# A fused attention and mixer kernel: the last group's output add split in two, its last two down-projection steps ordered by block, and a 64-row matmul operand widened to 128 rows with zeros

## The chip, the cores and the metric

The kernel runs on one core of one Trainium2 chip. The metric is the device time of one execution in microseconds (us), the median of several runs. The core has a matrix engine (TensorE, PE in the profile, with its weight loads shown apart as PEld), a vector engine (VectorE, DVE), a scalar engine (ScalarE, ACT), a general engine (GpSimd, POOL) and a queue that starts transfers (SyncE, SP). Every engine takes its own instructions in order and waits at semaphores for the others.

## The reference

Eight sequences of 576 tokens go through attention with 8 heads of 64 channels, four heads with a local mask of 32 tokens and four with a strided one, and then through two mixers:

```
x  = attention output, [8, 576, 512]
h  = relu(x^T @ w_tok1) @ w_tok2          # token mix: 576 -> 256 -> 576, over tokens
u  = x + h^T
h2 = relu(u @ w_ch1) @ w_ch2              # channel mix: 512 -> 1536 -> 512
out = u + h2
```

## The kernel before

**Precision.** Every matmul of the mixers is made of three. An operand `a` is held as a rounded part and a remainder, `ah + al`, both in a format that TensorE takes at one pass, and a product is `ah*bh + ah*bl + al*bh`. So names come in pairs: `t1h/t1l` are the weights of token mix 1, `w1h/w1l` and `w2h/w2l` those of the channel mix, `xh/xlo` are an activation, `uh/ul` are u, `gh/gl` the hidden layer. The rounded parts are written by ScalarE, the remainders by VectorE or GpSimd.

**Token mix 1 (`tok1`, L374).** For one sequence it contracts over the 576 tokens in `NSC` = 5 chunks of 128 rows. For each chunk, ScalarE makes `xh` (L384), VectorE `xlo` (L387), and TensorE does three matmuls for each of the two halves `m` of the 256 outputs (L396). The fifth chunk is short: 64 tokens are left. Its 64 rows of x are loaded twice, into rows 0 to 63 and 64 to 127. `t1l` holds for this chunk the rounded weights in its upper rows and the remainders in its lower rows, so that one matmul of 128 rows gives two of the three products; the third, rounded weights with `xlo`, is a matmul of 64 rows. `t1h` of that chunk has the rounded weights in all 128 rows, though only the first 64 are used there. It runs nine times: for sequence 0 in two halves of 256 columns, in the first part of the kernel, and for sequences 1 to 7 with 512 columns. ScalarE (`hh`, L400) and VectorE (`hl`, L404) read its result.

**Channel mix (`mlp`, L513).** The 8 x 576 tokens are taken in `NG` = 9 groups of 512. In a group, `up_proj` (L524) does 12 matmuls for each of `NFC` = 12 blocks `fc` of the hidden layer, ScalarE and VectorE make `gh` and `gl` (L528, L530), and `down_proj` (L538) adds 12 matmuls into the four accumulators `acc0` to `acc3`, one for each block of 128 output channels, all four in PSUM. At the end of a group the outputs are put together block by block (L559 to L563): VectorE adds acc and `uh` into a buffer `ot` of which there are two, then `ul` is added, by GpSimd or in the last group by VectorE, and SP stores the block of 256 KB.

**Order.** The first part of the kernel, with the conversion of the weights and group 0, follows an order written out by hand. After that the attention of the next sequences, their token mixes and the channel mix of the group before are woven together: functions are hung on half steps of the channel mix (`inserts`), and a scheduler that goes by its own time estimates and by priorities sets the final order on each engine. The strided attention runs as products on GpSimd (L342, L359) and sums on VectorE (L343, L361); its result goes through memory into `x`, of which there is one buffer. From group 7 on little but the channel mix is left.

Of the kernel before, what the change touches and what calls it, by code (L numbers as in the profile page):

```python
# [10 lines left out]
F32 = mybir.dt.float32  # L11
# [4 lines left out]
ALU = mybir.AluOpType  # L16
# [9 lines left out]
P = 128  # L26
# [6 lines left out]
NCC = DM // P  # L33
NFC = DF // P
NSC = 5
# [8 lines left out]
GT = 512  # L44
NG = B * S // GT
# [3 lines left out]
def attn_mixer_kernel(ctx, tc, qT, kT, vw, qs, ks, vs, qksT, vsP, mask, mask2, w1, w2, wt1, wt2, outT):  # L49
    nc = tc.nc  # L50
# [11 lines left out]
    w2h = const.tile([P, NFC, DM], F32R, name="w2h")  # L62
    w2l = const.tile([P, NFC, DM], F32R, name="w2l")

    t1h = const.tile([P, NSC, DT], F32R, name="t1h")
    t1l = const.tile([P, NSC, DT], F32R, name="t1l")
# [12 lines left out]
    def differ(name):  # L79
        return nc.gpsimd if name in ON_GPSIMD.split() else nc.vector  # L80


    def convert(name, srcs, n, cut):

        raw = stage.tile([P, DM, 2], U32, name="w_raw", bufs=3)
        for r0, c0, src in srcs:
            nr, w = src.shape
            nc.sync.dma_start(out=raw[r0:r0 + nr, c0:c0 + w].rearrange("p n t -> p (n t)"), in_=src.bitcast(U32))
        yield
        a = stage.tile([P, DM], U32, name="w_f", bufs=2)[:, :n]  # L90
        low, high = raw[:, :n, 0], raw[:, :n, 1]

        nc.scalar.activation(out=a.bitcast(F32), in_=high.bitcast(F32), func=AF.Abs, scale=REBIAS)
        if name in BY_VECTOR.split():
            yield
            nc.vector.tensor_scalar(out=a, in0=a, scalar1=3, scalar2=None, op0=ALU.logical_shift_left)
            nc.vector.scalar_tensor_tensor(out=a, in0=low, scalar=29, in1=a, op0=ALU.logical_shift_right, op1=ALU.bitwise_xor)
            nc.vector.scalar_tensor_tensor(out=a, in0=high, scalar=0x80000000, in1=a, op0=ALU.bitwise_and, op1=ALU.bitwise_xor)
        else:


            octets = raw.rearrange("p n t -> p (n t)").bitcast(U8).rearrange("p (n e) -> p n e", e=8)
            nc.scalar.copy(out=octets[:, :n, 4], in_=octets[:, :n, 3])
            yield
            nc.vector.tensor_scalar(
                out=high, in0=high, scalar1=5, scalar2=0x80000007, op0=ALU.arith_shift_right, op1=ALU.bitwise_and)
            nc.vector.scalar_tensor_tensor(out=a, in0=a, scalar=3, in1=high, op0=ALU.logical_shift_left, op1=ALU.bitwise_xor)
        yield
        yield from cut(a.bitcast(F32))

    def split(name, dsth, dstl, *srcs):
        c0, got = 0, []
        for src in srcs:
            got.append((0, c0, src))
            c0 += src.shape[1]

        def cut(f):
            if len(dsth.shape) == 3:
                f = f.rearrange("p (c n) -> p c n", c=dsth.shape[1])
            nc.scalar.copy(out=dsth, in_=f)  # L120
            yield
            differ(name).tensor_tensor(out=dstl, in0=f, in1=dsth.bitcast(F32), op=ALU.subtract)

        return convert(name, got, c0, cut)

    def t1_pieces():
        for c in range(0, NSC - 1, 2):
            yield split(f"t{c // 2}", t1h[:, c:c + 2], t1l[:, c:c + 2], *(wt1[P * i:P * i + P] for i in (c, c + 1)))

        def cut(f):  # L130
            nc.scalar.copy(out=t1h[:, NSC - 1], in_=f)
            nc.scalar.copy(out=t1l[:64, NSC - 1], in_=f[:64])
            yield
            differ("t2").tensor_tensor(out=t1l[64:, NSC - 1], in0=f[64:], in1=t1h[64:, NSC - 1].bitcast(F32), op=ALU.subtract)


        short = wt1[P * (NSC - 1):]
        yield convert("t2", [(0, 0, short), (64, 0, short)], DT, cut)
# [236 lines left out]
    def tok1(pool, banks, x_t, h, cs):  # L375

        n = cs.stop - cs.start
        ph = [b[:, cs] for b in banks]

        def chunk(c):  # L380
            short = c == NSC - 1
            x = x_t[:, c, cs]
            xh = pool.tile([P, DM], F32R, name="xh")[:, :n]
            nc.scalar.copy(out=xh, in_=x)  # L384
            yield
            xlo = pool.tile([P, DM], F32R, name="xlo")[:, :n]
            nc.vector.tensor_tensor(out=xlo, in0=x, in1=xh.bitcast(F32), op=ALU.subtract)  # L387
            yield
            for m in range(2):
                ms = slice(P * m, P * m + P)  # L390
                if short:
                    terms = ((t1h[:64, c, ms], xlo[:64]), (t1l[:, c, ms], xh))
                else:
                    terms = ((t1h[:, c, ms], xh), (t1h[:, c, ms], xlo), (t1l[:, c, ms], xh))
                for k, (l, r) in enumerate(terms):
                    nc.tensor.matmul(ph[m], l, r, start=(c == 0 and k == 0), stop=(short and k == 1), skip_group_check=True)  # L396

        def last():
            for m in range(2):
                nc.scalar.activation(out=h[m][0][:, cs], in_=ph[m], func=AF.Relu)  # L400
            yield
            for m in range(2):
                a, z = h[m][0][:, cs], h[m][1][:, cs]
                nc.vector.scalar_tensor_tensor(out=z, in0=ph[m], scalar=0.0, in1=a.bitcast(F32), op0=ALU.max, op1=ALU.subtract)  # L404

        return [chunk(c) for c in range(NSC)] + [last()]

    def new_h(pool):
        return [[pool.tile([P, DM], F32R, name=f"h{k}{m}", bufs=1) for k in "hl"] for m in range(2)]

    def new_u(pool):
        return [[pool.tile([P, GT], F32R, name=f"u{k}", bufs=NCC) for k in "hl"] for _ in range(NCC)]
# [30 lines left out]
    xp = ctx.enter_context(tc.tile_pool(name="xp", bufs=2))  # L443
# [37 lines left out]
    with tc.tile_pool(name="first", bufs=2) as first, \  # L481
# [4 lines left out]
        us = {0: new_u(xp)}  # L486
# [18 lines left out]
    up = ctx.enter_context(tc.tile_pool(name="up", bufs=3, reuse_waits="tile"))  # L505
# [4 lines left out]
    def run(g, n=100):  # L510
        for _ in range(n):
            next(g, None)

    def mlp(grp, us, inserts):
        acc = [ps_acc.tile([P, GT], F32, name=f"acc{cc}") for cc in range(NCC)]
        g = {}

        def up_proj(fc):
            fs = slice(P * fc, P * fc + P)
            ph = ps_h.tile([P, GT], F32, name="h")  # L520
            for cc in range(NCC):
                uh, ul = us[cc]
                for k, (l, r) in enumerate(((w1h, uh), (w1h, ul), (w1l, uh))):
                    nc.tensor.matmul(ph, l[:, cc, fs], r, start=(cc == 0 and k == 0), stop=(cc == NCC - 1 and k == 2))  # L524
            yield
            gh = up.tile([P, GT], F32R, name="gh")
            gl = up.tile([P, GT], F32R, name="gl")
            nc.scalar.activation(out=gh, in_=ph, func=AF.Relu)  # L528
            yield
            nc.vector.scalar_tensor_tensor(out=gl, in0=ph, scalar=0.0, in1=gh.bitcast(F32), op0=ALU.max, op1=ALU.subtract)  # L530
            g[fc] = (gh, gl)

        def down_proj(fc):
            gh, gl = g.pop(fc)
            for cc in range(NCC):
                cs = slice(P * cc, P * cc + P)
                for k, (l, r) in enumerate(((w2h, gh), (w2h, gl), (w2l, gh))):
                    nc.tensor.matmul(acc[cc], l[:, fc, cs], r, start=(fc == 0 and k == 0), stop=(fc == NFC - 1 and k == 2))  # L538
            yield

        if grp:
            run(up_proj(0))
            run(up_proj(1))
            for fc in range(NFC):
                if fc + 2 < NFC:
                    run(up_proj(fc + 2))
                for f in inserts.get(2 * fc, ()):
                    f()
                run(down_proj(fc))
                for f in inserts.get(2 * fc + 1, ()):  # L550
                    f()
        else:
            for fc in range(NFC):
                steps[f"A{fc}"], steps[f"D{fc}"] = up_proj(fc), down_proj(fc)
            in_order(ORDER.split("|")[1])
            for n, s in steps.items():
                assert next(s, steps) is steps, n
        for cc, (uh, ul) in enumerate(us):
            o_t = up.tile([P, GT], F32, name="ot", bufs=2)  # L559
            nc.vector.tensor_tensor(out=o_t, in0=acc[cc], in1=uh.bitcast(F32), op=ALU.add)  # L560
            add = nc.vector if grp == NG - 1 else nc.gpsimd
            add.tensor_tensor(out=o_t, in0=o_t, in1=ul.bitcast(F32), op=ALU.add)  # L562
            nc.sync.dma_start(out=outT[P * cc:P * cc + P, GT * grp:GT * grp + GT], in_=o_t)  # L563

    def do_load(b):
# [180 lines left out]
```

## Time and profile before

| what | value |
|---|---|
| median of 3 runs | 886.46 us (879.77, 886.46, 888.44) |
| the profiled execution, its own time | 882.51 us |
| its span, first to last instruction | 880.5 us |
| granted TensorE clock, mean | 0.982 |
| TensorE matmuls busy | 826.7 us, 94% of the span |
| VectorE busy | 487.8 us, 55% |
| GpSimd busy | 404.0 us, 46% |
| ScalarE busy | 208.5 us, 24% |

The profile is of one execution, and times within it are us from the first instruction. In a row of the timeline stand start, length, engine, line, operation, the tiles as out<-in, the shape, and in brackets how long the engine was idle before it and whom it waited for. The chain of waits is the work that ended last, followed back from the last instruction; a row has start, length, and engine with line, and xN where N instructions in a row are put together. A matmul's end in the profile is modelled, so its pace is read from the distance of the starts.

### The profile page before, as it was taken

The page shows a single profiled execution, that of the slowest core. Times are in us where ns is not written, and L with a number is a line of the kernel's source. Part 1 is how long each engine was busy: PE and PEld are TensorE (multiplying, and loading weights), DVE is VectorE, ACT ScalarE, POOL GpSimd, SP SyncE. Part 2 cuts the span into 40 slices and gives each one's busy share as a digit, 9 for nine tenths or more (in the row PEclk, how much of TensorE's full clock was granted, in tenths as well). Part 3 has the DMA queues.
Part 4 walks back from the last instruction along what each step waited for, and adds up shares of the span by engine and source line. Part 5 has one row for each costly group of instructions (what it writes and reads, how often), then busy time and mean ns, then how long its engine had stood idle before and what let it go on. Part 6 is the DMA issues. An engine that isn't in the chain of part 4 may idle for free.

```text
span 880.5 us, 16250 instructions
## 1 busy us (share of the span) xinstructions
PE 826.7 (94%) x6820; PEld 659.7 (75%) x6820; DVE 487.8 (55%) x941; ACT 208.5 (24%) x378; POOL 404.0 (46%) x385
## 2 busy tenths in 40 slices
PE   4588999799978999999999999999999999999996
PEld 3366787578856787787887887778788877888885
DVE  4789873667567755775577567645774222112112
ACT  3676652221112212211212112112111121111110
POOL 0112300786577765795679477845885002002000
PEclk9979999999998999999999999999999999999998
DMA  7647754302542323023402421223112001001001
GB/s 256 198 157 251 240 191 123 130 1 92 132 160 63 102 54 123 28 80 88 157 28 79 142 97 40 74 64 115 35 53 77 11 1 48 1 1 41 8 1 48
DMA packets 57639, 78.99 MB, mean 90 GB/s; under 512 B 18144, under 2 KB 39776, under 8 KB 57568
## 3 DMA queue, kind: packets, MB, share of 16 engines
q1 hardware_dynamic: 57568, 77.97, 27.5%
q8 instruction: 53, 0.87, 0.4%
q14 instruction: 18, 0.15, 0.1%
HBM read 59.54 MB, written 18.28 MB: 88 GB/s over the span
## 4 chain that ended last, share of the span: by engine, by line
PE 65%; POOL 13%; DVE 9%; DMA 7%; issue 2%; SPq 2%; ACT 1%; DVEq 0%; POOLq 0%; ACTq 0%
PE h L524 25%; PE acc L538 23%; POOL sprod L342 9%; PE t L433 6%; POOL sprod L359 4%; PE t L396 4%; DMA sb<-in_ks 3%; PE t L427 3%; DVE ss L343 2%; DMA lk<-in_kT 1%; PE t L207 1%; DVE xlo L387 1%; PE t L170 1%; SPq L372 1%; DMA xs<-sb 1%
## 5 line engine op out<-in xcount | busy, mean ns | idle before, releaser
L342 POOL TENSOR_TENSOR sprod<-sb,sa 128x576 f32<-128x576 f32 (+6 forms) x162 | 175.1, 1110 | 133.8 <-DMA sb<-in_ks 114.8
L359 POOL TENSOR_TENSOR sprod<-sa,ss 128x448 f32<-128x448 f32 (+7 forms) x162 | 162.9, 1038 | 34.3 <-DVE ss L352 24.9
L524 PE MATMUL h<-ul,w1h 128*128 128x512 f32 x432 | 170.7, 395 | 0.0
L524 PE MATMUL h<-uh,w1l 128*128 128x512 f32 x432 | 169.5, 392 | 0.0
L538 PE MATMUL acc<-gh,w2l 128*128 128x512 f32 x432 | 169.3, 392 | 0.0
L524 PE MATMUL h<-uh,w1h 128*128 128x512 f32 x432 | 168.4, 396 | 0.9 <-DVE gl L530 0.9
L538 PE MATMUL acc<-gl,w2h 128*128 128x512 f32 x432 | 168.7, 390 | 0.0
L538 PE MATMUL acc<-gh,w2h 128*128 128x512 f32 x432 | 165.6, 394 | 0.2 <-ACT gh L528 0.2
L530 DVE SCALAR_TENSOR_TENSOR gl<-h,gh 128x512 fp32r<-128x512 f32 x108 | 74.0, 686 | 141.5 <-ACT gh L528 141.3
L528 ACT ACTIVATE gh<-h 128x512 fp32r<-128x512 f32 x108 | 64.4, 599 | 317.7 <-PE h L524 304.3
L343 DVE TENSOR_REDUCE ss<-sprod 128x9 f32<-128x576 f32 (+6 forms) x162 | 90.8, 570 | 55.4 <-POOL sprod L342 54.3
L361 DVE TENSOR_REDUCE sb<-sprod 128x64 f32<-128x64 f32 (+8 forms) x162 | 91.4, 571 | 36.9 <-POOL sprod L359 35.9
L562 POOL TENSOR_TENSOR ot<-ot,ul 128x512 f32<-128x512 f32 x32 | 41.2, 1295 | 136.5 <-DVE ot L560 136.4
L524 PEld LDWEIGHTS h<-uh,w1h 128*128 128x128 f32 x432 | 81.0, 188 | 18.4 <-DVE gl L530 1.4
L538 PEld LDWEIGHTS acc<-gh,w2h 128*128 128x128 f32 x432 | 81.2, 188 | 17.6 <-ACT gh L528 0.7
L524 PEld LDWEIGHTS h<-uh,w1l 128*128 128x128 f32 x432 | 81.6, 189 | 16.7
L524 PEld LDWEIGHTS h<-ul,w1h 128*128 128x128 f32 x432 | 81.4, 189 | 16.8
L538 PEld LDWEIGHTS acc<-gh,w2l 128*128 128x128 f32 x432 | 81.1, 188 | 17.1
L538 PEld LDWEIGHTS acc<-gl,w2h 128*128 128x128 f32 x432 | 81.1, 188 | 16.3
L387 DVE TENSOR_TENSOR xlo<-x,xh 128x512 fp32r<-128x512 f32 (+1 forms) x45 | 40.0, 905 | 33.8 <-ACT xh L384 33.7
L438 DVE TENSOR_TENSOR ul<-t,uh 128x512 fp32r<-128x512 f32 (+7 forms) x64 | 28.8, 454 | 42.6 <-ACT uh L436 42.4
L436 ACT CAST uh<-t 128x512 fp32r<-128x512 f32 (+7 forms) x64 | 25.5, 399 | 108.8 <-PE t L433 108.7
(97 smaller groups left out, 881.0 us busy)
## 6 DMA issues: line engine op xcount, KB each, us to landing
w_raw<-in_w SPq DMA_DIRECT2D x24, 512.0 KB
out_t<-ot SPq DMA_DIRECT2D x36, 256.0 KB
lv<-in_vw SPq DMA_DIRECT2D x8, 520.0 KB
x<-xs SPq DMA_DIRECT2D x8, 512.0 KB
lv<-in_vw SPq DMA_DIRECT2D x6, 650.0 KB
xl<-lx SPq DMA_DIRECT2D x14, 256.0 KB
x<-xl SPq DMA_DIRECT2D x7, 512.0 KB
sa<-in_qs SPq DMA_DIRECT2D x6, 576.0 KB
```

What stands on the lines that cost most here:

```text
L342: nc.gpsimd.tensor_tensor(out=pr, in0=k_t[:, n0:n0 + n], in1=q_t[:, i:i + 1].to_broadcast([P, n, D]), op=ALU.mult)
L343: nc.vector.tensor_reduce(out=s_t[:, i, n0:n0 + n], in_=pr, axis=AX.X, op=ALU.add)
L359: nc.gpsimd.tensor_tensor(out=pr, in0=v_t[:, d0:d0 + nd, :n], in1=s_t[:, i:i + 1, :n].to_broadcast([P, nd, n]), op=ALU.mult)
L361: nc.vector.tensor_reduce(out=o_t[:, i, d0:d0 + nd], in_=pr, axis=AX.X, op=ALU.add)
L387: nc.vector.tensor_tensor(out=xlo, in0=x, in1=xh.bitcast(F32), op=ALU.subtract)
L396: nc.tensor.matmul(ph[m], l, r, start=(c == 0 and k == 0), stop=(short and k == 1), skip_group_check=True)
L433: nc.tensor.matmul(pu[:, :n], l[:, cs], r[:, m, t0:t1], start=False, stop=(m == 1 and k == 2), skip_group_check=True)
L524: nc.tensor.matmul(ph, l[:, cc, fs], r, start=(cc == 0 and k == 0), stop=(cc == NCC - 1 and k == 2))
L528: nc.scalar.activation(out=gh, in_=ph, func=AF.Relu)
L530: nc.vector.scalar_tensor_tensor(out=gl, in0=ph, scalar=0.0, in1=gh.bitcast(F32), op0=ALU.max, op1=ALU.subtract)
L538: nc.tensor.matmul(acc[cc], l[:, fc, cs], r, start=(fc == 0 and k == 0), stop=(fc == NFC - 1 and k == 2))
L562: add.tensor_tensor(out=o_t, in0=o_t, in1=ul.bitcast(F32), op=ALU.add)
```

## The change

It has three parts.

One: the conversion of `w_tok1`'s short chunk sets the lower 64 rows of `t1h` to zero after `t1l` has been made from them, and `tok1` then takes all 128 rows of `t1h` and of `xlo` for the third product. The lower rows add zero times x. The number of matmuls stays as it is.

Two: in the last group u is put together ahead of the end, `whole = uh + ul`, one VectorE operation a block at steps 4 to 7. At the end one operation a block adds acc to it, in place, and the store reads from there. `whole` takes the place of the buffer of `x`, which has all four blocks, so no block waits for the store of another.

Three: in the last group the down-projection of the last two steps, `fc` 10 and 11, is one call that goes through the accumulators one after the other, both steps for each.

```diff
@@ conversion of w_tok1, cut() of the short chunk
             differ("t2").tensor_tensor(out=t1l[64:, NSC - 1], in0=f[64:], in1=t1h[64:, NSC - 1].bitcast(F32), op=ALU.subtract)
+            differ("t2").memset(t1h[64:, NSC - 1].bitcast(F32), 0.0)
@@ tok1
                 if short:
-                    terms = ((t1h[:64, c, ms], xlo[:64]), (t1l[:, c, ms], xh))
+                    terms = ((t1h[:, c, ms], xlo), (t1l[:, c, ms], xh))
@@ mlp
-        def down_proj(fc):
-            gh, gl = g.pop(fc)
+        def down_proj(*fcs):
+            gs = [g.pop(fc) for fc in fcs]
             for cc in range(NCC):
                 cs = slice(P * cc, P * cc + P)
-                for k, (l, r) in enumerate(((w2h, gh), (w2h, gl), (w2l, gh))):
-                    nc.tensor.matmul(acc[cc], l[:, fc, cs], r, start=(fc == 0 and k == 0), stop=(fc == NFC - 1 and k == 2))
+                for fc, (gh, gl) in zip(fcs, gs):
+                    for k, (l, r) in enumerate(((w2h, gh), (w2h, gl), (w2l, gh))):
+                        nc.tensor.matmul(acc[cc], l[:, fc, cs], r, start=(fc == 0 and k == 0), stop=(fc == NFC - 1 and k == 2))
...
-                run(down_proj(fc))
+                if grp < NG - 1 or fc < NFC - 2:
+                    run(down_proj(fc))
+                elif fc == NFC - 2:
+                    run(down_proj(fc, fc + 1))
...
+                if grp == NG - 1 and 4 <= fc < 4 + NCC:
+                    if fc == 4:
+                        whole = xp.tile([P, NSC, GT], F32, name="x", bufs=1)
+                    uh, ul = (u.bitcast(F32) for u in us[fc - 4])
+                    nc.vector.tensor_tensor(out=whole[:, fc - 4], in0=uh, in1=ul, op=ALU.add)
...
         for cc, (uh, ul) in enumerate(us):
-            o_t = up.tile([P, GT], F32, name="ot", bufs=2)
-            nc.vector.tensor_tensor(out=o_t, in0=acc[cc], in1=uh.bitcast(F32), op=ALU.add)
-            add = nc.vector if grp == NG - 1 else nc.gpsimd
-            add.tensor_tensor(out=o_t, in0=o_t, in1=ul.bitcast(F32), op=ALU.add)
+            if grp == NG - 1:
+                o_t = whole[:, cc]
+                nc.vector.tensor_tensor(out=o_t, in0=acc[cc], in1=o_t, op=ALU.add)
+            else:
+                o_t = up.tile([P, GT], F32, name="ot", bufs=2)
+                nc.vector.tensor_tensor(out=o_t, in0=acc[cc], in1=uh.bitcast(F32), op=ALU.add)
+                nc.gpsimd.tensor_tensor(out=o_t, in0=o_t, in1=ul.bitcast(F32), op=ALU.add)
             nc.sync.dma_start(out=outT[P * cc:P * cc + P, GT * grp:GT * grp + GT], in_=o_t)
```

The scheduler decides where these instructions stand, and it did not keep the order of the code in part three. First TensorE, the last twelve matmuls of the program. The numbers are the program's: `gh_8569` belongs to the last step, `fc` 11. Before:

```order
L538 MATMUL acc0_8257<-gh_8569,w2h_69 128x512
L538 MATMUL acc1_8258<-gh_8569,w2h_69 128x512
L538 MATMUL acc0_8257<-gl_8570,w2h_69 128x512
L538 MATMUL acc0_8257<-gh_8569,w2l_70 128x512
L538 MATMUL acc1_8258<-gl_8570,w2h_69 128x512
L538 MATMUL acc1_8258<-gh_8569,w2l_70 128x512
L538 MATMUL acc2_8259<-gh_8569,w2h_69 128x512
L538 MATMUL acc2_8259<-gl_8570,w2h_69 128x512
L538 MATMUL acc2_8259<-gh_8569,w2l_70 128x512
L538 MATMUL acc3_8260<-gh_8569,w2h_69 128x512
L538 MATMUL acc3_8260<-gl_8570,w2h_69 128x512
L538 MATMUL acc3_8260<-gh_8569,w2l_70 128x512
```

The same twelve places of the changed kernel, where `gh_8546` is step 10 and `gh_8575` step 11:

```order
L540 MATMUL acc2_8260<-gh_8575,w2h_69 128x512
L540 MATMUL acc3_8261<-gl_8547,w2h_69 128x512
L540 MATMUL acc0_8258<-gl_8576,w2h_69 128x512
L540 MATMUL acc0_8258<-gh_8575,w2l_70 128x512
L540 MATMUL acc1_8259<-gl_8576,w2h_69 128x512
L540 MATMUL acc1_8259<-gh_8575,w2l_70 128x512
L540 MATMUL acc2_8260<-gl_8576,w2h_69 128x512
L540 MATMUL acc2_8260<-gh_8575,w2l_70 128x512
L540 MATMUL acc3_8261<-gh_8546,w2l_70 128x512
L540 MATMUL acc3_8261<-gh_8575,w2h_69 128x512
L540 MATMUL acc3_8261<-gl_8576,w2h_69 128x512
L540 MATMUL acc3_8261<-gh_8575,w2l_70 128x512
```

Counted from the last matmul as 0, the accumulators are complete at 8, 6, 3 and 0 before, and at 8, 6, 4 and 0 in the changed kernel. Only acc2 moved, by one place.

Second, VectorE at the end of the program, where the outputs are put together. Before:

```order
L530 SCALAR_TENSOR_TENSOR gl_8570<-h_8556,gh_8569 128x512
L560 TENSOR_TENSOR ot_8609<-acc0_8257,uh_7892 128x512
L560 TENSOR_TENSOR ot_8613<-acc1_8258,uh_7894 128x512
L562 TENSOR_TENSOR ot_8609<-ot_8609,ul_7893 128x512
L562 TENSOR_TENSOR ot_8613<-ot_8613,ul_7895 128x512
L560 TENSOR_TENSOR ot_8617<-acc2_8259,uh_7896 128x512
L560 TENSOR_TENSOR ot_8621<-acc3_8260,uh_7898 128x512
L562 TENSOR_TENSOR ot_8617<-ot_8617,ul_7897 128x512
L562 TENSOR_TENSOR ot_8621<-ot_8621,ul_7899 128x512
```

The changed kernel there:

```order
L531 SCALAR_TENSOR_TENSOR gl_8576<-h_8562,gh_8575 128x512
L573 TENSOR_TENSOR x_8441<-acc0_8258,x_8441 128x512
L573 TENSOR_TENSOR x_8441<-acc1_8259,x_8441 128x512
L573 TENSOR_TENSOR x_8441<-acc2_8260,x_8441 128x512
L573 TENSOR_TENSOR x_8441<-acc3_8261,x_8441 128x512
```

Eight operations after the last `gl` became four, and each of them waits for TensorE alone; before, the third and fourth L560 also waited for the stores of the first two blocks.

Third, VectorE where the four new additions went. They do not stand in the last group but one group earlier, in group 7, around the last `ul` of token mix 2. Before:

```order
L530 SCALAR_TENSOR_TENSOR gl<-h,gh 128x512 x2
L438 TENSOR_TENSOR ul<-t,uh 128x512
L530 SCALAR_TENSOR_TENSOR gl<-h,gh 128x512
L438 TENSOR_TENSOR ul<-t,uh 128x512 x2
L530 SCALAR_TENSOR_TENSOR gl<-h,gh 128x512
L438 TENSOR_TENSOR ul<-t,uh 128x512
L530 SCALAR_TENSOR_TENSOR gl<-h,gh 128x512 x8
```

In the changed kernel:

```order
L531 SCALAR_TENSOR_TENSOR gl<-h,gh 128x512 x2
L439 TENSOR_TENSOR ul<-t,uh 128x512
L531 SCALAR_TENSOR_TENSOR gl<-h,gh 128x512
L439 TENSOR_TENSOR ul<-t,uh 128x512 x2
L531 SCALAR_TENSOR_TENSOR gl<-h,gh 128x512
L563 TENSOR_TENSOR x<-uh,ul 128x512 x3
L439 TENSOR_TENSOR ul<-t,uh 128x512
L563 TENSOR_TENSOR x<-uh,ul 128x512
L531 SCALAR_TENSOR_TENSOR gl<-h,gh 128x512 x8
```

The first of the four waits for TensorE to have read `x` for the last time, and the last `ul` and eight `gl` stand behind it. On GpSimd the new memset stands right behind the subtraction for `t1l`'s lower rows (L134), and TensorE's first short-chunk matmul waits for it. Every other instruction stands on its engine as before.

## The prediction

> **What bounds the kernel now.** I read the page first, for the busy shares and the chain of waits by engine; then the pieces of that chain in order of time, to see where TensorE sets the end and where not; then the timeline at the two places that the change touches.
>
> ```profile
> PE 826.7 (94%) x6820; PEld 659.7 (75%) x6820; DVE 487.8 (55%) x941; ACT 208.5 (24%) x378; POOL 404.0 (46%) x385
> PE 65%; POOL 13%; DVE 9%; DMA 7%; issue 2%; SPq 2%; ACT 1%; DVEq 0%; POOLq 0%; ACTq 0%
> ```
>
> TensorE is busy for 94% of the span, but only 65% of the chain is TensorE's; GpSimd, VectorE and transfers carry 29%. So time taken from TensorE counts only in the stretches where the chain is TensorE's. At the very end the chain is no longer TensorE's either:
>
> ```profile
> 870.37 0.39 PE L538 MATMUL acc<-gh,w2l 128*128 128x512 f32 x1
> 872.18 0.39 PE L538 MATMUL acc<-gh,w2l 128*128 128x512 f32 x1
> 870.85 1.29 DVE L560 TENSOR_TENSOR ot<-acc,uh 128x512 f32<-128x512 f32 x2 [5.08 <-PE acc L538]
> 872.05 1.28 DVE L562 TENSOR_TENSOR ot<-ot,ul 128x512 f32<-128x512 f32 x2
> 874.89 1.31 DVE L560 TENSOR_TENSOR ot<-acc,uh 128x512 f32<-128x512 f32 x2 [1.55 <-DMA out_t<-ot]
> 876.12 1.28 DVE L562 TENSOR_TENSOR ot<-ot,ul 128x512 f32<-128x512 f32 x2
> 872.76 2.00 DMA out_t<-ot
> 872.50:879.50 7.00, 0.07 (x1) 0.00 (x0) 3.35 (x6) 0.00 (x0) 0.00 (x0) 0.73 0.39 150
> ```
>
> The last matmul starts at 872.18. VectorE does two blocks, then stands idle for 1.55 us until a store (2.00 us) frees one of the two buffers, and does the other two. It ends at 876.12 + 1.28 = 877.40, and the span of 880.5 ends 3.1 us later: the last store, and the program's close.
>
> The other place is the short chunk of token mix 1. This is sequence 7's, first TensorE's matmuls, then its weight loads, then line L396 in five windows, and a piece of the chain for the ordinary pace:
>
> ```profile
> 709.94 0.39 PE L524 MATMUL h<-ul,w1h 128*128 128x512 f32 x1
> 710.26 0.50 PE L396 MATMUL t<-xlo,t1h 64*128 64x512 f32 x1
> 710.69 0.49 PE L396 MATMUL t<-xh,t1l 128*128 128x512 f32 x1
> 711.11 0.50 PE L396 MATMUL t<-xlo,t1h 64*128 64x512 f32 x1
> 711.54 0.50 PE L396 MATMUL t<-xh,t1l 128*128 128x512 f32 x1
> 711.87 0.39 PE L524 MATMUL h<-uh,w1l 128*128 128x512 f32 x1
> 710.68 0.19 PEld L396 LDWEIGHTS t<-xh,t1l 128*128 128x128 f32 x1 [0.25 <-issue]
> 712.10 0.19 PEld L524 LDWEIGHTS h<-ul,w1h 128*128 128x128 f32 x1
> sum 9.66, PE 8.07 PEld 3.69; mean PE 1.61 PEld 0.74
> 766.49 2.72 PE acc L538 x12
> ```
>
> Twelve ordinary matmuls take 2.72 us, 0.227 each. Around the 64-row matmuls the starts lie 0.32, 0.43, 0.42, 0.43 and 0.33 apart. The loads show why: in the ordinary stream a load stands a whole matmul ahead of its own (the one at 712.10 runs beside the matmul that starts there, for the next), but the load of 710.68 starts with its matmul, after 0.25 us in which nothing was loaded. Between a 64-row and a 128-row operand the load does not run ahead, four times a place and a little less at the edges. The sum row is of five such places (sequences 3 to 7), each from the start of the last ordinary matmul before to that of the first one after, five distances: 9.66 / 5 = 1.93 us where 5 x 0.227 = 1.13 would stand. So a place costs **0.80 us** of TensorE.
>
> **The change, part by part.** *The end.* acc0 is complete with the ninth matmul from the last, as before, and VectorE started 870.85 - 870.37 = 0.48 after that matmul's start. The four remaining operations read what L560 read in one operand and SBUF in the other, and pairs of them start 0.6 apart (the two at 870.85 fill 1.29, the second lasting 0.68). So they start at 870.85, 871.46, 872.06 and, for acc3, 872.18 + 0.48 = 872.66, and end at 873.35. That is 877.40 - 873.35 = 4.05 us earlier. What comes behind is the same but for the stores: four now follow each other 0.6 us apart. In the 7 us of the windows' row the transfer engines were busy for a share of 0.39, which is 2.73 us for four stores, 0.68 each; the last may wait for 3 x 0.08 = 0.2 us or so. I take **3.9 us**. Bounds: 3.4 if it waits for a whole store, 4.05 if for none. The store queue is free, since SP has nothing else there. That two steps now alternate on an accumulator costs nothing that a row shows: the stream at 766.49 has three matmuls in a row on each accumulator at the ordinary pace, and the last step's `gh` and `gl` are not asked for earlier than the 14th matmul from the end, 3.0 us before the last start, while the last `gl` of before started at 865.08:
>
> ```profile
> 865.08 0.69 DVE L530 SCALAR_TENSOR_TENSOR gl<-h,gh 128x512 fp32r<-128x512 f32 x1 [4.75 <-ACT gh L528]
> 753.81 0.69 DVE L530 SCALAR_TENSOR_TENSOR gl<-h,gh 128x512 fp32r<-128x512 f32 x1 [1.97 <-ACT gh L528]
> 754.27 0.88 PE t L427 x5
> 755.16 1.59 PE t L433 x6
> 761.72 0.69 DVE L530 SCALAR_TENSOR_TENSOR gl<-h,gh 128x512 fp32r<-128x512 f32 x1 [3.56 <-ACT gh L528]
> 38.36 0.94 POOL L134 TENSOR_TENSOR t1l<-w_f,t1h 64x256 fp32r<-64x256 f32 x1 [7.06 <-ACT t1h L131]
> 48.57 1.54 POOL L122 TENSOR_TENSOR w1l<-w_f,w1h 128x512 fp32r<-128x512 f32 x1 [9.28 <-ACT w1h L120]
> 51.05 0.38 PE L396 MATMUL t<-xlo,t1h 64*128 64x256 f32 x1 [0.62 <-DVE xlo L387]
> ```
>
> *The four additions in advance.* They stand behind the `gl` of 753.81 and wait for TensorE's last reading of `x`, the transposes that end at 755.15, or, if the wait is put at the end of the six matmuls behind them, at about 756.7. Three times 0.69 (L562's pace on VectorE) then end at 757.2 to 758.8; behind them wait the last `ul` and the `gl` of 761.72, before which VectorE was idle for 3.56 us. I cost them at nothing. Their cover goes if they start after about 759.5; then TensorE would be late by what is over.
>
> *The memset.* The subtraction of 38.36 is followed on GpSimd by 9.28 us of idleness, and the first matmul that needs the zeros starts at 51.05, held by VectorE. No row shows a memset of this shape; between 0 and the 0.94 of the subtraction of the same 64x256, either is hidden. I take nothing.
>
> *The short chunk.* If 128 rows put it at the ordinary pace, 0.80 us is saved at each of seven places, and something in the two halves of sequence 0. What of it reaches the end is read from the chain:
>
> ```profile
> 60.77 0.42 DVE L404 SCALAR_TENSOR_TENSOR hl<-t,hh 128x256 fp32r<-128x256 f32 x1 [0.39 <-ACT hh L400]
> 168.83 0.69 DVE ot L560
> 270.45 5.80 PE t L396 x14
> 355.43 1.71 PE t L396 x4
> 442.38 12.59 POOL sprod L342 x9
> 471.63 0.61 DVE gl L530
> 531.08 11.77 POOL sprod L342 x8
> 633.41 1.71 PE t L396 x4
> 450.63:452.57 1.94, 1.62 (x4) 0.74 (x4) 1.00 0.04 8
> 541.32:543.25 1.93, 1.61 (x4) 0.74 (x4) 1.00 0.00 0
> ```
>
> Sequences 2, 3, 6 and 7 have their short chunk on the chain (270.45, 355.43, 633.41, and the matmuls of 710.26, where the chain is TensorE's to the end): 4 x 0.80 = 3.2 us. Sequence 1's lies at 168 us, where VectorE waits for a store with its `ot` (168.83) and the next `hl` stands behind that: nothing. Sequences 4 and 5 have theirs in the windows from 450.63 and 541.32, in the stretches where GpSimd's products carry the chain (442.38, 531.08); TensorE would come sooner to the next wait for VectorE (471.63): nothing. At the end of sequence 0's `tok1` the chain goes on over ScalarE and VectorE, which waited there for 0.39 us (60.77): 0.4. Together **3.6 us**. The bounds: 0, or all of it, 7 x 0.80 = 5.6 and for sequence 0 up to twice 0.80, 7.2.
>
> The sum: 3.9 + 3.6 = **7.5 us**. Against the profiled execution's own 882.51 that is 875.0; the median of the runs shown stands 3.95 above that execution, and from 886.46 it is **879.0 us**, 0.85% faster.
>
> The Trainium skill ("TensorE: Matmul & The Clock Gate", The mechanism) says that a weight load runs beside matmuls in flight only when the two use different row groups of the array. By that rule a 128-row load after a 128-row matmul would be the one that can't run ahead; the row of 712.10 shows it running ahead, so the trace speaks against the rule in this form. By the rule the short chunk would gain nothing and the sum would be 3.9; it is the second rival.
>
> **The rivals.** *All of the chunk's gain arrives.* The chain alternates between engines, and a GpSimd stretch that starts earlier because TensorE came earlier gives everything back to it. Then 3.9 + 7.2 = 11.1: 875.4. Against it, the waits at 471.63 and 168.83, which TensorE's being early does not move.
>
> *The chunk gains nothing.* The gaps could belong to something other than the 64 rows, such as the alternation of `xlo` and `t1l` operands in two halves. For it, the edges of the place (0.32 and 0.33) lie between 128-row operands and 64-row ones and are not doubled. Against it, the ordinary chunks alternate in the same way without a gap. It gives 886.46 - 3.9 = 882.6.
>
> *Slower: VectorE's stretched operations.* An `xlo` on the chain is several times as long as its line's median:
>
> ```profile
> 267.37 3.04 DVE xlo L387
> L387 DVE TENSOR_TENSOR xlo<-x,xh x45: 409/691/3026, 36.2 to 705.1; 128x512 fp32r<-128x512 f32 x35, 128x256 fp32r<-128x256 f32 x10
> ```
>
> The median is 0.69, the longest 3.03: it lies beside a product on GpSimd, and both read SBUF. The change shifts these two engines against each other by up to a microsecond. If four more operations on the chain came to lie so, each 3.03 - 0.69 = 2.3 us longer, they would take 9.4 and the result would be 886.46 - 7.5 + 9.4 = 888.4. It decides from the fourth on (7.5 / 2.3 = 3.2). The one that is there could as well go, for 2.3 us more gain. The Trainium skill ("SBUF — State Buffer", SBUF: two separate sides) says that VectorE with two SBUF inputs and GpSimd take a shared pair of ports in turn, whole instructions at a time; these rows agree, and by it no such operation would wait longer than one product, which gives no other sum.
>
> **How the numbers follow.** My forecast, with some tenths to either side in both terms, has a chance of 0.58; all of the chunk 0.2; nothing of it 0.13; slower 0.04; 0.05 is left for what I don't see. A difference of about 1%, 8.9 us, is what a measurement of this kernel can tell from no change: the three runs of before span 8.7 us by themselves. Faster by more means below 877.6. The second case (875.4) mostly lies there, and the forecast's 879.0 falls there in some two of five measurements, since medians vary by a few us: 0.37 in all. Slower by more needs over 895.3: 0.02. The range takes in 875.4 and 882.6 with some 3 us of the runs' own spread outside of each: 872.5 to 885.0.
>
> **What would show it.** At the end: VectorE's four operations back to back behind TensorE's last matmul, no wait for a store, the span's end some 4.4 us after the last matmul's start, where it was 8.3. At the short chunk: five distances of 0.227 instead of 1.93 in all, and the load's idle gaps gone. In the middle: longer waits of TensorE near 471 us, as the part of the gain that is lost. I would be wrong if the gaps stay with 128 rows, if the last store waits, or if the stretches on GpSimd between 200 and 560 us come out longer or shorter by more than the 3.6 us that I argue about.

## The result, and the profile after

The changed kernel takes 876.48 us (median of 8 runs, 874.11 to 880.02) where the kernel before took 883.49 (8 runs, 879.77 to 888.44): a ratio of 0.993, 95% interval 0.9907 to 0.9953. By the medians that is 7.0 us less, by the ratio 6.2 (4.2 to 8.2); the forecast was 7.5, to 879.0 from the 886.46 shown then. That the result lies 2.5 us below 879.0 comes from the kernel before, whose median is 3.0 us lower with five more runs. The profiled execution took 876.04 us, its span 874.3 where it was 880.5.

The page's busy times and the chain by engine:

```profile
PE 820.2 (94%) x6820; PEld 659.0 (75%) x6820; DVE 486.2 (56%) x941; ACT 207.4 (24%) x378; POOL 404.1 (46%) x386
PE 58%; POOL 16%; DVE 11%; DMA 7%; SPq 3%; issue 3%; ACT 1%; POOLq 0%; DVEq 0%; ACTq 0%
```

TensorE is busy 6.5 us less with as many instructions. Its share of the chain is 58% where it was 65%, but that says nothing of the change: a second execution of the kernel before, which comes further below, has 59%.

The end, in the timeline of TensorE, VectorE and the store queue, and in one window that holds the four stores:

```profile
869.95 0.39 PE L540 MATMUL acc<-gh,w2l 128*128 128x512 f32 x1
868.56 2.50 DVE L573 TENSOR_TENSOR x<-acc,x 128x512 f32<-128x512 f32 x4 [5.03 <-PE acc L540]
869.28 2.14 SPq L578 DMA_DIRECT2D out_t<-x  x4
868.00:874.00 6.00, 2.33 (x11) 1.60 (x9) 2.50 (x4) 0.00 (x0) 0.00 (x0) 1.00 0.45 175
```

VectorE's four additions stand back to back, begin while TensorE is still at acc2 and acc3, and end at 871.06, 1.1 us after the last matmul's start. The span ends 4.3 us after that start, where it was 8.3. The transfer engines are busy for 0.45 x 6 = 2.7 us, as before, now all in one stretch.

The short chunk of sequence 7, TensorE's matmuls and two of the weight loads:

```profile
708.51 0.39 PE L525 MATMUL h<-ul,w1h 128*128 128x512 f32 x1
708.73 0.39 PE L397 MATMUL t<-xlo,t1h 128*128 128x512 f32 x1
708.96 0.39 PE L397 MATMUL t<-xh,t1l 128*128 128x512 f32 x1
709.18 0.39 PE L397 MATMUL t<-xlo,t1h 128*128 128x512 f32 x1
709.41 0.39 PE L397 MATMUL t<-xh,t1l 128*128 128x512 f32 x1
709.64 0.39 PE L525 MATMUL h<-uh,w1l 128*128 128x512 f32 x1
708.74 0.19 PEld L397 LDWEIGHTS t<-xh,t1l 128*128 128x128 f32 x1
708.96 0.19 PEld L397 LDWEIGHTS t<-xlo,t1h 128*128 128x128 f32 x1
```

Five distances take 709.64 - 708.51 = 1.13 us where they took 1.93, and the loads run beside the matmul before their own.

What was costed at nothing, in the changed kernel: the memset, the additions in advance, and the `gl` behind them.

```profile
L135 POOL MEMSET t1h<- x1: 306/306/306, 40.0 to 40.0; 64x256 f32 x1
752.96 1.90 DVE L563 TENSOR_TENSOR x<-uh,ul 128x512 f32<-128x512 f32 x3 [0.69 <-PE t L428]
755.23 0.69 DVE L439 TENSOR_TENSOR ul<-t,uh 128x512 fp32r<-128x512 f32 x1 [0.38 <-ACT uh L437]
759.48 0.69 DVE L531 SCALAR_TENSOR_TENSOR gl<-h,gh 128x512 fp32r<-128x512 f32 x1 [2.83 <-ACT gh L529]
```

The memset took 0.31 us at 40 us, 11 us ahead of its first use. The additions began with the last transposes, were done before the last `ul` wanted VectorE, and the next `gl` still found it idle for 2.83 us.

### The profile page after: what moved, and what is told of

It reads as the page before. It is cut to its first block, busy times and chain, and to the rows that moved or that the text cites. A ratio compares the mean times of both kernels' runs of the same rounds, so it can differ in the third digit from the quotient of the medians.

```text
span 874.3 us, 16247 instructions
## 1 busy us (share of the span) xinstructions
PE 820.2 (94%) x6820; PEld 659.0 (75%) x6820; DVE 486.2 (56%) x941; ACT 207.4 (24%) x378; POOL 404.1 (46%) x386
## 4 chain that ended last, share of the span: by engine, by line
PE 58%; POOL 16%; DVE 11%; DMA 7%; SPq 3%; issue 3%; ACT 1%; POOLq 0%; DVEq 0%; ACTq 0%
PE h L525 24%; PE acc L540 21%; POOL sprod L343 11%; PE t L434 5%; DMA sb<-in_ks 4%; POOL sprod L360 4%; PE t L428 2%; DVE ss L344 2%; PE t L397 2%; DMA xs<-sb 1%; SPq L373 1%; DMA lk<-in_kT 1%; POOL ot L577 1%; DVE xlo L388 1%; PE t L208 1%
```

## The experiments

### The two halves of the change by themselves

The short chunk alone (the memset and the one line in `tok1`, all else as before), timed twice, and the end alone (the other two parts).

> Part one alone: the short chunk of token mix 1 in 128 rows, the last group as before. My theory: each of the seven places with 512 columns loses its 0.80 us (five distances of 0.227 us), about half of it reaches the end, so the program is 2 to 4 us shorter than before (ratio 0.995 to 0.998), and the stretch from the last matmul's start to the span's end stays at 8.3 us. If all of it arrives: 6 to 7 us (0.992). If the gaps belong to the alternation of operands and not to the 64 rows: no difference, and distances of 0.43 us remain.

> Part one alone once more, since its first timing (ratio 0.9989, interval 0.9965 to 1.0014) and its first trace (TensorE's last matmul starts 2.8 us earlier than in the first trace of before) do not say the same. If the short chunk is worth the 3.6 us of the forecast, the ratio is 0.996; if an `xlo` that VectorE finishes late at sequence 6 takes back 1.3 us in most executions, 0.9975; if nothing arrives, 1. At the five calm places of the trace five distances must again take 1.13 us, or more only where VectorE's `xlo` is waited for.

> Parts two and three alone: u in advance and the last two steps in pairs, the short chunk with 64 rows as before. My theory: 3.9 to 4.0 us shorter (ratio 0.9955), all of it behind the last matmul: 4.4 us from its start to the span's end instead of 8.3. The rival, that the changed placing of the buffer shifts the middle as well, would show as another time of TensorE at the start of the last group, beyond the 1 us or so by which two executions differ.

| kernel | median us | ratio to before | 95% interval |
|---|---|---|---|
| short chunk alone, first | 880.58 | 0.9989 | 0.9965 to 1.0014 |
| short chunk alone, second | 879.82 | 0.995 | 0.9927 to 0.9972 |
| end alone | 877.54 | 0.9958 | 0.993 to 0.9985 |
| the whole change | 876.48 | 0.993 | 0.9907 to 0.9953 |

The end alone is worth 0.0042 x 883 = 3.7 us by the ratio, and 4.0 in the trace. The short chunk looks like the smaller half, and its two timings differ: 1.0 us, less than expected and not told apart from no change, and 4.4 us, in the mean 2.7. What the whole change has above the end's 4.0 is 7.0 - 4.0 = 3.0 by the medians and 6.2 - 4.0 = 2.2 by the ratio. In the traces of the short chunk alone the five distances take 1.13 us again, except where an `xlo` of VectorE is waited for.

### The end taken apart

Three kernels. The advance without the pairing (`run(down_proj(fc))` for every step), the pairing without the advance, and the kernel before with four buffers in place of two but still two operations a block:

```diff
-            o_t = up.tile([P, GT], F32, name="ot", bufs=2)
+            if grp == NG - 1 and cc == 0:
+                whole = xp.tile([P, NSC, GT], F32, name="x", bufs=1)
+            o_t = whole[:, cc] if grp == NG - 1 else up.tile([P, GT], F32, name="ot", bufs=2)
```

> Part two without part three and part one: u in advance, the last two steps in the order of the code as before. My theory: the stretch from the last matmul's start to the span's end is 4.4 us, the same as with part three, since the accumulators are complete at 8, 6, 3 and 0 matmuls from the last one already. If part three matters, it is longer by a tenth or more.

> Part three alone: the last two steps in one call, accumulator by accumulator, the outputs put together in two operations and two buffers as before. My theory: nothing at the end, 8.3 us from the last matmul's start to the span's end, with the 1.5 us wait for a store.

> The kernel before with four buffers for the last group's outputs in place of two, still two operations a block. It takes the wait for the store away and leaves the eight operations. My theory: VectorE's eight operations stand back to back from 0.5 us before the third block is complete; 8 x 0.61 to 0.65 = 5.0 us after 870.85 on the clock of before, so the end is 1.5 us earlier (6.8 us from the last matmul's start), and of the change's 4.0 us the wait is 1.5 and the operations 2.5. If the store was what set the end, 3 us or more are gained here.

From the last matmul's start to the span's end: 4.31 us with the advance alone, 8.33 with the pairing alone, 6.62 with four buffers; before it was 8.33, with the whole change 4.31. Each of the three has one execution, but this stretch hardly varies: 8.32 or 8.33 in all five executions with the end as before or with the pairing alone, and 4.31 or 4.32 in all with the advance. The timelines of VectorE, first of the advance alone, then of the pairing alone, then of the four buffers with the last matmul:

```profile
869.71 2.50 DVE L569 TENSOR_TENSOR x<-acc,x 128x512 f32<-128x512 f32 x4 [5.02 <-PE acc L539]
```

```profile
873.88 1.30 DVE L565 TENSOR_TENSOR ot<-acc,uh 128x512 f32<-128x512 f32 x2 [1.55 <-DMA out_t<-ot]
```

```profile
872.74 1.29 DVE L562 TENSOR_TENSOR x<-acc,uh 128x512 f32<-128x512 f32 x2 [5.03 <-PE acc L538]
873.95 0.68 DVE L564 TENSOR_TENSOR x<-x,ul 128x512 f32<-128x512 f32 x1
...
876.35 1.28 DVE L564 TENSOR_TENSOR x<-x,ul 128x512 f32<-128x512 f32 x2
874.13 0.39 PE L538 MATMUL acc<-gh,w2l 128*128 128x512 f32 x1
```

So the whole gain of the end is the advance's. The pairing does nothing there: the wait of 1.55 us for a store is there with it, and the advance has its 2.50 us without it. Of the 4.02 us the wait for the store was 8.33 - 6.62 = 1.71, since eight operations without it still end at 877.63, 3.5 us after the last matmul's start; the four operations that went are the other 2.31. Four buffers alone would have brought less than half.

### What stops the weight load

The changed kernel with 64 rows in both products of the short chunk; it leaves out the product with the remainders of these weights:

```diff
-                    terms = ((t1h[:, c, ms], xlo), (t1l[:, c, ms], xh))
+                    terms = ((t1h[:64, c, ms], xlo[:64]), (t1l[:64, c, ms], xh[:64]))
```

> The changed kernel, but the short chunk's second product reads 64 rows too (the remainders of its weights are left out): four 64-row matmuls in a row instead of a change of height between each. If a 64-row operand can never be loaded ahead, all five distances stay near 0.43 and the place takes 1.9 us. If the change from 64 to 128 rows is what stops the load, only the edges are long: about 0.32 at the entry, 0.33 at the exit and 0.227 between, 1.33 us a place. My theory is the change of height.

Sequence 7's place, matmuls and then two loads:

```profile
708.62 0.39 PE L525 MATMUL h<-ul,w1h 128*128 128x512 f32 x1
708.94 0.49 PE L397 MATMUL t<-xlo,t1h 64*128 64x512 f32 x1
709.28 0.39 PE L397 MATMUL t<-xh,t1l 64*128 64x512 f32 x1
709.51 0.39 PE L397 MATMUL t<-xlo,t1h 64*128 64x512 f32 x1
709.75 0.39 PE L397 MATMUL t<-xh,t1l 64*128 64x512 f32 x1
710.07 0.50 PE L525 MATMUL h<-uh,w1l 128*128 128x512 f32 x1
710.41 0.40 PE L525 MATMUL h<-uh,w1h 128*128 128x512 f32 x1
709.28 0.18 PEld L397 LDWEIGHTS t<-xlo,t1h 64*128 64x128 f32 x1
710.07 0.19 PEld L525 LDWEIGHTS h<-uh,w1l 128*128 128x128 f32 x1 [0.37 <-issue]
```

Between 64 rows and 64 rows the distances are 0.23 and 0.24, the pace of 128-row operands, and the load of 709.28 runs ahead, beside the matmul before its own. Only at the entry and at the exit the load stands still; the load of 710.07 starts with its matmul. The place takes 710.07 - 708.62 = 1.45 us, between 1.93 and 1.13. (The expected 1.33 left out that the distance behind an entry is long as well, 0.34.) The distance behind the exit, to 710.41, is also 0.34, where it was ordinary with mixed heights; with it two changes cost 710.41 - 708.62 - 6 x 0.227 = 0.43 us. So it is the change of height, not the 64 rows: four changes cost 0.80 us, two cost 0.43, some 0.2 us each.

### Which sequences' savings arrive

Two versions of the changed kernel in which only some sequences take the short chunk in 128 rows (a flag in `tok1`: sequences 1, 4 and 5, or 0, 2, 3, 6 and 7), and both kernels profiled once more, to see how far two executions lie apart.

> The changed kernel, but only sequences 1, 4 and 5 take the short chunk in 128 rows; 0, 2, 3, 6 and 7 take 64 as before. My theory: these three places lie beside waits for VectorE and GpSimd, so the 2.4 us that TensorE saves are lost in longer waits, and what is left is the gain of the end alone: 4 us (ratio 0.9955). If all of TensorE's saving arrives: 6.4 us (0.9928).

> The changed kernel, but sequences 1, 4 and 5 take the short chunk in 64 rows as before; 0, 2, 3, 6 and 7 take 128. My theory: the same time as the whole change, 7 us under before (ratio 0.992), since nothing that 1, 4 and 5 save arrives. If all arrives, 2.4 us longer than the whole change. Sequences 6 and 7 alone, where the chain is TensorE's to the end, must give 1.6 us whatever happens before.

> The kernel before, profiled once more, to see how far two executions of one program lie apart in the middle: my theory is that TensorE's instructions between 150 and 560 us differ by 1 us or more between executions with nothing changed, and that the end (8.3 us) and the distances at the short chunk (1.93 us) do not.

> The changed kernel, profiled once more, for the same: the end 4.4 us, the short chunk 5 x 0.227 us, and TensorE's lead over the kernel before at the start of the last group between 1.6 us (sequences 6 and 7 alone) and 4 us, other than the 2.2 us of its first profile.

By time the two can't be told apart: 0.9954 (0.9926 to 0.9982) for 1, 4 and 5, and 0.9943 (0.9919 to 0.9967) for the others, where 0.9955 and 0.992 were expected. The traces give the point where TensorE starts its last matmul, ahead of which the end plays no part:

| executions | last matmul's start, us |
|---|---|
| 64 rows everywhere: before twice, pairing, four buffers, end alone, advance | 872.2, 873.5, 871.2, 874.1, 875.3, 871.1; mean 872.9 |
| 128 rows everywhere: chunk alone twice, the change twice | 869.4, 872.2, 870.0, 867.6; mean 869.8 |
| 128 rows in sequences 1, 4, 5 | 871.5 |
| 128 rows in sequences 0, 2, 3, 6, 7 | 869.2 |

The mean lead is 872.9 - 869.8 = 3.1 us, but executions of one program lie up to 2.8 us apart (the chunk alone: 869.4 and 872.2). The second execution of the changed kernel leads by 4.6 to 5.9 us, more than the 4 us that were expected at most. The end alone starts its last matmul 3.1 us later than the first execution of before, which would fit the rival that the buffer's new place shifts the middle; but the advance alone, with the same place, starts it 1.1 us earlier, so this too is spread. The two selections fall where the theory put them, 1, 4 and 5 nearer to the first row and the others to the second; one execution of each doesn't settle it.

One cause of the spread shows in the traces, at the short chunks of sequences 5 and 6; here sequence 6, at 630 us. First the second execution of before, then the short chunk alone (first), each with TensorE's first short-chunk matmul, the first matmul behind the place and VectorE's `xlo`, the latter with GpSimd's products beside it; then the changed kernel's `xlo` and products:

```profile
634.67 0.50 PE L396 MATMUL t<-xlo,t1h 64*128 64x512 f32 x1 [1.36 <-DVE xlo L387]
636.29 0.39 PE L524 MATMUL h<-ul,w1h 128*128 128x512 f32 x1
632.13 2.49 DVE L387 TENSOR_TENSOR xlo<-x,xh 128x512 fp32r<-128x512 f32 x1
```

```profile
631.87 0.50 PE L397 MATMUL t<-xlo,t1h 128*128 128x512 f32 x1 [1.32 <-DVE xlo L388]
632.91 0.40 PE L525 MATMUL h<-ul,w1h 128*128 128x512 f32 x1
629.29 2.53 DVE L388 TENSOR_TENSOR xlo<-x,xh 128x512 fp32r<-128x512 f32 x1
622.70 8.57 POOL L343 TENSOR_TENSOR sprod<-sb,sa 128x384 f32<-128x384 f32 x6
```

```profile
631.08 1.11 DVE L388 TENSOR_TENSOR xlo<-x,xh 128x512 fp32r<-128x512 f32 x1
623.13 11.78 POOL L343 TENSOR_TENSOR sprod<-sb,sa 128x576 f32<-128x576 f32 x8
```

In some executions this `xlo` gets its turn between two products and takes 1.11 us; in others it waits until the run of products is over (622.70 + 8.57 = 631.27, and `xlo` ends at 631.82), takes 2.5 us, and TensorE waits for it, 0.3 to 1.4 us in the executions that have it. That can be more than the 0.80 that the place saves. The saving itself mostly stays: from the late `xlo`'s end to the matmul behind the place it is 636.29 - 634.62 = 1.67 us with 64 rows and 632.91 - 631.82 = 1.09 with 128, 0.6 less. It happened with 64 rows and with 128, so it needs no change of the kernel. With 64 rows everywhere the `xlo` of sequence 5 was late in five of six executions and that of sequence 6 in four; with 128 rows everywhere each was late in one of four. Whether the change makes it rarer is open with so few.

The granted clock goes with the spread as well: over the 62 timings of before that have it on record (0.970 to 0.990), 0.01 less of it goes with some 3.6 us more. By that slope the mean clocks of these (0.981) and of the changed kernel's eight timings (0.985) would make 1.2 us of the difference; this is an estimate, and no run holds the clock fixed.

What was expected of the two second executions held at the end (8.32 and 4.32 us) and at the short chunks of sequences 3, 4 and 7 (1.93 and 1.13), but not at those of sequences 5 and 6 of before, which take 3.30 and 3.36 us with the late `xlo` where the first execution had 1.93. Between 150 and 560 us the two executions of before lie up to 3.4 us apart.

### The same for token mix 2

The transposes of x in `tok2` (L428 in the changed kernel) also change between 128 and 64 rows. Where the bank has room, whole blocks of 128 rows are transposed, and the half that isn't wanted lands in columns that nobody reads:

```diff
+        lead = t0 % P
+        whole_rows = lead + n + (-(lead + n)) % P <= 512
+        o = lead if whole_rows else 0
...
+            if whole_rows:
+                q = o + t - t0 - r
+                nc.tensor.matmul(pu[:, q:q + P], x_t[:, c, cs], ident,
+                                 is_transpose=True, start=(t == t0), stop=False, skip_group_check=True)
...
+        pu = pu[:, o:o + n]
```

> The changed kernel, and the same done to token mix 2: its transposes of 64 rows of x are replaced, where the bank has room, by transposes of whole blocks of 128 rows whose other half lands in columns that nobody reads (56 of 64 of them). In the trace of the changed kernel a transpose of 64 rows stretches the distance ahead of it from 0.227 to 0.32 and its own to 0.20 where a 128-row one has 0.11. My theory: 0.2 us each, 11 us of TensorE, of which about half arrives: 4 to 7 us under the changed kernel (ratio to before 0.984 to 0.988). If a transpose differs from a matmul and the rows don't matter: no difference to the changed kernel (0.993). If everything else takes it back: less than 2 us.

It takes 871.49 us (6 runs, 868.75 to 872.97), a ratio of 0.9873 to before, 0.9839 to 0.9906: 5.0 us under the changed kernel's median, and the fastest of all that were run. First its page's busy row, its transposes of whole blocks and those that stayed; then the changed kernel's transposes of 64 rows:

```profile
PE 810.4 (93%) x6820; PEld 659.7 (76%) x6820; DVE 486.2 (56%) x941; ACT 207.6 (24%) x378; POOL 405.6 (47%) x386
L431 PE MATMUL t<-ident,x 128*128 128x128 f32 x156 | 27.8, 279 | 4.4 <-DVE ul L448 2.3 <-DVE hl L405 2.0
L436 PE MATMUL t<-ident,x 64*128 64x64 f32 x8 | 2.2, 272 | 0.0
```

```profile
L428 PE MATMUL t<-ident,x 64*128 64x64 f32 x64 | 16.7, 270 | 0.0
```

With 56 of the 64 gone, TensorE is busy 820.2 - 810.4 = 9.8 us less, 0.18 us for each (11.8 us less than in the second execution of the changed kernel, 0.21 for each), and about half of it arrives, as with the short chunk.

## Why the prediction was right, point by point

**The end** was right in its parts. Forecast 3.9 us, measured 4.0; VectorE's four operations were to fill 870.85 to 873.35, 2.50 us, and fill 2.50. The last store was to wait for about 0.2 us; from VectorE's last operation to the span's end it is 3.2 us where it was 3.1, so 0.1. That the pairing does nothing was read from the order of the matmuls, and holds.

**The short chunk's 0.80 us a place** was right, and so was its cause by the load's idle gaps. The prediction named it "between a 64-row and a 128-row operand", and the kernel with 64 rows in both products shows just that. The Trainium skill's sentence on row groups ("TensorE: Matmul & The Clock Gate", The mechanism), by which a load overlaps a matmul in flight only where the row groups differ, came out the other way: loads ran ahead from 128 to 128 rows and from 64 to 64, over the same rows of the operands, and stood still where the height changed. The same section also lets a load go ahead into a background weight buffer; whether these loads did, no trace here shows. The rival that hung on the sentence, no gain, is excluded for TensorE by the five distances of 1.13 us, and for the time by the second timing of the short chunk alone (interval 0.9927 to 0.9972).

**What of it arrives** was the less certain term: 3.6 us forecast, 3.1 by the mean of the traces, 3.0 or 2.2 by the times of the whole change. The sum came near, but its parts are off against each other, so that is partly luck. For sequences 0 to 5 the forecast put 0.4 + 1.6 = 2.0 us by 570 us; TensorE's start of the same matmul there is at 570.1 in the mean of the six executions with 64 rows and at 569.1 in the four with 128. That 1.0 is smaller than the spread of either (568.7 to 571.4, 567.3 to 571.9). For sequences 6 and 7 it put 1.6; behind sequence 7's place the means are 712.6 and 709.5, so these two brought 3.1 - 1.0 = 2.1, some of it because fewer executions with 128 rows had the late `xlo`. That a saving in the middle is lost again shows in the means for sequence 4: the lead is 0.6 us behind its place (452.6 and 452.0) and gone ahead of sequence 5's (541.6 and 541.6). But sequence 3's, which was counted in full, is gone as well ahead of sequence 4's (450.7 and 450.9). The step that was too simple is to read from the chain of one execution which places count: that execution is the only one of the six with 64 rows in which neither sequence 5's nor sequence 6's `xlo` was late. The choice of sequences is borne out only in its sum.

**The rivals.** All of the gain arriving (11.1 us in all) lies outside the interval of the ratio, which ends at 0.0093 x 883 = 8.2 us. The slower one named a mechanism that exists, an `xlo` stretched by products, and priced it at 2.3 us; it is there with and without the change, as a matter of chance, and cost TensorE up to 1.4 us at a place, not four times over. The prediction's side remark that by the Trainium skill's rule of the shared ports ("SBUF — State Buffer", SBUF: two separate sides) an operation would wait for one product at most is refuted by the row that it stands under: 3.04 us with 0.69 of its own leave 2.3 of waiting, and GpSimd does the rest of an addition and two products (2.08 us together) in that time. The section says that whoever starts first keeps the ports for the whole instruction; in this case's traces the one that waits doesn't always get the next turn.

## What to carry to other kernels

Where TensorE's stream changes the height of its operands, fill the short one up with zeros, or read a whole block and leave the surplus unread: each change of height cost 0.2 us here, and the rows cost nothing. At a program's end, count the operations that stand behind the last matmul and what their buffers wait for; whatever doesn't need that matmul's result can be done ahead, and it brought more than more buffers would have. A chain of waits from one execution says which places can count, but not how often they do: profile a second execution before trusting a place whose margin is a microsecond.

## What the runs showed of the hardware that was not expected

A 64-row operand is as fast as one of 128 rows as long as its neighbours have 64 rows too (0.23 us for 512 columns); the cost is in the change, about 0.2 us each way, and 64-row transposes among taller ones cost as much (0.18 to 0.21 us for each of the 56 that went). VectorE's operation with two operands in SBUF can be passed over by a run of GpSimd products: the same instruction at the same place took 1.11 us in one execution and 2.53 in another, by how it fell between them.
